# Half-tile staggered layer-norm pipeline, w1 in quarters, and segment sums taken from transposed pairs on VectorE

## The chip, the cores and the metric

The kernel runs on one core of one Trainium2 chip. The metric is the device time of one execution in microseconds (us), the median over several runs; smaller is better.

A core has five engines that work side by side, each in the order of its own instruction list: PE (TensorE, matrix products; its weight loads are shown apart as PEld), DVE (VectorE), ACT (ScalarE), POOL (GpSimd) and SP (SyncE, which here issues transfers). Transfers run on 16 DMA engines. Products are written to PSUM, a small memory that DVE and ACT read; everything else works in SBUF. An engine waits for another by a semaphore, and what stands behind a waiting instruction on the same engine waits as well.

## What is computed

The reference takes x (2048 tokens by 1024, bf16), normalises each token to xn, and adds two branches to x:

```python
xn = _layernorm(x)
return x + _A_ref(xn, A_mem0, A_Wq, A_Wk, A_Wv, A_Wo, A_seg_len) + _B_ref(xn, B_w1, B_w2, B_w3, B_w4)
```

Branch B is a mixer: h = gelu(layernorm(xn) @ w1); four groups of channels of h are shifted by one or two tokens and multiplied by w2; x1 = xn + that; then x1 + gelu(layernorm(x1) @ w3) @ w4, with 3584 inner channels.

Branch A is attention with 32 heads of 128 over segments of 32 tokens. Each segment is processed together with 8 memory rows, which are the output of the attention for the memory rows of the segment before it. So branch A is a recurrence over 64 segments. The kernel breaks it: it guesses the memory rows (attention is so flat here that a row's output is close to the mean of the values, which needs only the sum of xn over each segment, times Wv and Wo), runs all segments in parallel with the guess, and checks at the end that the guess agrees with the result within a tolerance. Otherwise a slow serial version runs.

## The kernel before

The order of the work on PE, SP and POOL is that of the program text all through; in the first two stages that of DVE and ACT is too. The line numbers here and in the profile are those of the kernel before. The stages, with the time at which PE does them in the profiled execution:

- **Stage 1, h = gelu(layernorm(xn) @ w1), 10.3 to 75.8 us.** The 2048 tokens are 16 tiles `n` of 128. SP loads x tiles (`load_x`, L226; a ring of 7) and w1 in two halves of 1 MB (L231) in the order x0, x1, half, x2, half, x3 to x6, then w2 (L236). For each tile, `norm_stats` computes mean and variance on DVE (two `bn_stats`, L249 and L252, `bn_aggr`, L253, and two small operations, L254 and L255), and POOL raises to the power of -1/2 (L256). `norm2` (L264) makes the doubly normalised tile on DVE for the first `NPE` = 8 tiles; these are transposed on PE (`transposes`, L283, four products with an identity per half tile) and copied from PSUM by ACT (L287) or, for the second half of tile 0, by DVE (L285). For tiles 8 to 15 ACT does `norm2` (L266) and SP transposes by DMA (L267). `norm1` (L273) makes xn, which POOL writes to a scratch tensor in DRAM (`xn_scratch`, L274). `seg_sums` (L292) then multiplies xn by a 128x4 matrix of ones to sum the segments of 32 tokens, eight products per tile on PE and a copy on ACT (L293). `stage1` (L300) makes for each of 8 output blocks `co` a sum of 8 products, and ACT applies gelu (L302); `between` hangs transposes, `prep` (norm2, statistics, norm1) and segment sums behind blocks `co`. It takes tile 0 alone, tile 1 alone, and then seven pairs. 13 products with a tile of zeros (L317) run ahead of all this.
- **Stage 2, the shifted product with w2 and the next layer norm, 75.9 to 131.1 us** (L387; DMA transposes at L400).
- **Stage 3, the two products with w3 and w4, 131.1 to 543 us.** Four blocks `tb` of 512 tokens: 28 blocks of channels against w3 (L523), then for each of 4 token tiles 56 products against w4 (L548) and an addition of R1 (L549), a tile that SP loads (`load_r1`, L514, L515) and to which POOL first adds x (L544). At its beginning SP issues m0 (the 8 memory rows, L412), the last four pieces of w3 (L205), w4 in seven pieces of 1 MB (L416), and the first R1. PE makes the guess of the memory rows in between: `mem_start` (L425, after block 20 of the first w3 pass) puts m0 in place and adds its rows' sum to that of segment 0; `unit_vb` (L440) multiplies 71 columns (8 copies for the first memory rows, 63 further segments) by Wv, `unit_g` (L454) by Wo, 256 products each.
- **Values for branch A (L579), 543 to 764 us, and attention, 764 us to the end**: projections (L652), scores (L667), outputs (L691), and the output projection `Out.piece` (L710), 32 products of 512 columns for each chunk, an addition on DVE (L716) and a store (L717). Eight chunks are left for the end; the last two are stored from SP.

Of the kernel before, what the change touches and what calls it, by code (L numbers as in the profile page):

```python
# [77 lines left out]
def kernel(  # L78
# [47 lines left out]
    segsum_np = np.zeros((P, 4), np.float32)  # L126
    for t in range(P):
        segsum_np[t, t // SEG] = 1.0
    segsum = const_tile("c_segsum", segsum_np)
# [54 lines left out]
    with tc.manual_schedule(engines={mybir.EngineType.PE, mybir.EngineType.SP, mybir.EngineType.Pool}), ExitStack() as actx:  # L184
# [6 lines left out]
        with ExitStack() as bctx:  # L191
            w3ctx = bctx.enter_context(ExitStack())
            xctx = bctx.enter_context(ExitStack())
            xsum = xctx.enter_context(tc.tile_pool(name="xs", bufs=1)).tile([P, KT, NSEG], BF16)
# [12 lines left out]
            with ExitStack() as hctx:  # L207
# [7 lines left out]
                with ExitStack() as p0:  # L215
# [13 lines left out]
                    load_x(1)  # L229
                    for c in range(2):  # L230
                        nc.sync.dma_start(w1_sb[:, :, c * 512:(c + 1) * 512], w1_v[:, :, c * 512:(c + 1) * 512])  # L231
                        load_x(c + 2)
                    for n in range(4, 7):
                        load_x(n)
# [54 lines left out]
                    def seg_sums(n, xn):  # L289
                        ps = psum0.tile([P, KT, 4], F32, tag="xs")  # L290
                        for k in range(KT):
                            nc.tensor.matmul(ps[:, k, :], xn[:, k * P:(k + 1) * P], segsum[:], start=True, stop=True)  # L292
                        nc.scalar.copy(xsum[:, :, 4 * n:4 * n + 4], ps[:])  # L293

                    def stage1(n0, nt, xn2T, between):
                        w = nt * P
                        for co in range(KT):
                            ps = psum.tile([P, 512], F32, tag="mm", bufs=4)
                            for k in range(KT):
                                nc.tensor.matmul(ps[:, :w].rearrange("p (n t) -> p n t", t=P), w1_sb[:, k, co * P:(co + 1) * P],  # L300
                                                 xn2T[:, :nt, k, :], start=(k == 0), stop=(k == KT - 1))
# [14 lines left out]
                    for i in range(13):  # L316
                        nc.tensor.matmul(ps[:], wz[:, :P], wz[:], start=(i == 0), stop=(i == 12))  # L317
                    norm_stats(0)
                    norm_stats(1, 0)
                    t0 = xn2T_tile()  # L320
                    xn2 = norm2(0, t0, 0)
                    transposes(xn2, t0, 0, 0)
                    transposes(xn2, t0, 0, 1, on_dve=True)
# [3 lines left out]
                    t1 = xn2T_tile()  # L327
                    xn2 = norm2(1, t1, 0)
                    norm_stats(2)

                    def first(xn2=xn2, t1=t1):
                        transposes(xn2, t1, 0, 0)
                        transposes(xn2, t1, 0, 1)
                    xns = {}

                    def sums_of(n):
                        if n in xns:
                            seg_sums(n, xns.pop(n))

                    stage1(0, 1, t0, {3: [first], 4: [lambda: norm_stats(3)]})  # L340
                    groups = [(1, 1)] + [(n, 2) for n in range(2, NT, 2)]
                    tiles2 = {1: t1}
                    xn2s = {}

                    def prep(n):
                        xn2s[n] = norm2(n, tiles2[n - n % 2], n % 2)
                        norm_stats(n + 2)
                        done = range(n - 2, n - 1) if n < NPE else range(NPE - 2, n + 1) if n == NPE else range(n, n + 1)
                        for m in done:
                            xns[m] = norm1(m)  # L350

                    def tr(n, half):
                        transposes(xn2s[n], tiles2[n - n % 2], n % 2, half)


                    for gi, (n0, nt) in enumerate(groups):
                        between = {c: [] for c in range(KT)}
                        if gi + 1 < len(groups) and groups[gi + 1][0] < NPE:
                            m0 = groups[gi + 1][0]
                            tiles2[m0] = xn2T_tile()  # L360
                            prep(m0)
                            between[1] += [lambda m0=m0: tr(m0, 0), lambda m0=m0: prep(m0 + 1)]
                            between[2] += [lambda m0=m0: tr(m0, 1)]
                            between[5] += [lambda m0=m0: tr(m0 + 1, 0)]
                            between[6] += [lambda m0=m0: tr(m0 + 1, 1)]
                        if gi + 2 < len(groups) and groups[gi + 2][0] >= NPE:
                            m0 = groups[gi + 2][0]
                            tiles2[m0] = xn2T_tile()
                            between[2] += [lambda m0=m0: prep(m0)]
                            between[5] += [lambda m0=m0: prep(m0 + 1)]  # L370
                        between[3] += [lambda n0=n0: sums_of(n0 - 1)]
                        between[4] += [lambda n0=n0: sums_of(n0 - 2)]
                        stage1(n0, nt, tiles2[n0], between)
# [443 lines left out]
        for o in rest[-2:]:  # L817
            o.last = True
# [178 lines left out]
```

## Time and profile before

| | us |
|---|---|
| median of 8 runs | 1530.63 |
| lowest, highest | 1529.32, 1531.52 |
| the profiled execution, its own time | 1529.74 |
| its span, first to last instruction | 1527.8 |
| PE busy (share of the span) | 1513.7 (99%) |
| DVE, ACT, POOL busy | 529.8, 506.6, 178.5 |
| mean granted TensorE clock | 0.998 of full |

The span is what the trace covers; 1.9 us of the execution's own time lie around it. Since PE is nearly always busy, the sums of the whole run say little: one has to look at the places where PE is idle, where its clock is down, and at what PE does that could be left out. A line of the timeline has start, duration, engine, line, operation, output <- inputs, and at its end, in square brackets, how long the engine had been idle and what ended that. Several instructions of one kind are merged (x8). The ends of products are modelled, so merged products can look some tenths of a us longer than their stream; the distance from one start to the next is the safer number. The chain of waits has start, duration, what. "SPq" is SP's issuing of transfers; the transfer itself comes later.

### The profile page before, as it was taken

How to read it: one execution, taken by the hardware profiler on the slowest of the kernel's cores; microseconds unless marked ns; L12 is line 12 of the kernel's file. 1: busy time of each engine (PE TensorE's matmuls, PEld its weight loads, DVE VectorE, ACT ScalarE, POOL GpSimd, SP SyncE). 2: the span in 40 equal slices, each digit the busy share in tenths (PEclk: the TensorE clock that was granted, in tenths of full speed). 3: DMA queues.
4: the chain of work that ended last, by engine and by line, in shares of the span. 5: the costliest groups of instructions: out<-in, count | busy, mean ns of one | idle time of the engine just before them, and what ended most of it. 6: DMA issues, size and time to landing. Idle time of an engine off the chain costs nothing.

```text
span 1527.8 us, 24314 instructions
## 1 busy us (share of the span) xinstructions
PE 1513.7 (99%) x9810; PEld 811.0 (53%) x9883; DVE 529.8 (35%) x1131; ACT 506.6 (33%) x1155; POOL 178.5 (12%) x248
## 2 busy tenths in 40 slices
PE   8999999999999999999999999999999999999998
PEld 7844444444444444444466645654665555445554
DVE  7284010000210122211146624650664266426641
ACT  5633202103012011111156614650663266326620
POOL 5232020221211222100000010001000100010001
PEclk9999999999999999999999999999999999999999
DMA  7779543452352877632499947992997398728711
GB/s 247 190 213 310 214 150 126 134 185 96 110 177 83 209 260 252 225 128 78 129 240 249 235 133 183 236 235 80 235 242 189 106 232 218 183 80 202 177 46 51
DMA packets 287373, 270.03 MB, mean 177 GB/s; under 512 B 136875, under 2 KB 255040, under 8 KB 287000
## 3 DMA queue, kind: packets, MB, share of 16 engines
q1 hardware_dynamic: 265208, 185.79, 47.1%
q0 software_dynamic: 22048, 82.63, 15.5%
q8 instruction: 80, 1.31, 0.4%
q14 instruction: 37, 0.30, 0.1%
HBM read 190.98 MB, written 46.19 MB: 155 GB/s over the span
## 4 chain that ended last, share of the span: by engine, by line
PE 98%; DMA 1%; DVE 0%; issue 0%; ACT 0%; SPq 0%
PE ps L652 30%; PE ps L579 14%; PE pso L710 14%; PE ps L523 13%; PE ps L548 13%; PE ps L387 4%; PE ps L300 3%; PE psS L667 2%; PE psO L691 2%; DMA xt<-in_A_x_dram 1%; PE ps L474 1%; PE ps L837 1%; PE gps L454 1%; PE ps L440 1%; PE ps L292 0%
## 5 line engine op out<-in xcount | busy, mean ns | idle before, releaser
L652 PE MATMUL ps<-hTb,wt 128*128 128x396 bf16 (+3 forms) x2560 | 509.5, 343 | 0.0
L652 PEld LDWEIGHTS <-wt 128*128 128x128 bf16 x2560 | 234.2, 98 | 166.1
L710 PE MATMUL pso<-wo_sb,oX 128*128 128x512 bf16 x1001 | 223.4, 379 | 1.3 <-issue 0.2
L579 PE MATMUL ps<-wt,xT 128*128 128x512 bf16 x1004 | 220.1, 379 | 1.1
L523 PE MATMUL ps<-xn3T,w_sb 128*128 128x512 bf16 x896 | 195.7, 379 | 0.0
L548 PE MATMUL ps<-w_sb,h3T 128*128 128x512 bf16 x872 | 194.3, 379 | 1.2
L579 PEld LDWEIGHTS <-xT 128*128 128x128 bf16 x1024 | 100.2, 98 | 120.8
L524 ACT ACTIVATE h3T<-ps 128x512 bf16<-128x512 f32 x112 | 66.8, 597 | 292.1 <-PE ps L523 291.2
L710 PEld LDWEIGHTS <-oX 128*128 128x128 bf16 x1024 | 98.8, 98 | 115.3
L658 ACT CAST KT<-ps 128x396 bf16<-128x396 f32 (+3 forms) x160 | 82.3, 514 | 223.7 <-PE ps L652 222.4
L548 PEld LDWEIGHTS <-h3T 128*128 128x128 bf16 x896 | 86.8, 98 | 102.8
L523 PEld LDWEIGHTS <-w_sb 128*128 128x128 bf16 x896 | 86.8, 98 | 102.7
L673 DVE TENSOR_REDUCE sums<-sm 99x4 f32<-99x396 f32 (+2 forms) x176 | 97.6, 555 | 113.5 <-ACT sm L671 113.5
L669 DVE TENSOR_TENSOR sm<-psS,c_mask_reg_sb 99x396 f32<-99x396 f32 x160 | 91.2, 570 | 90.0 <-PE psS L667 89.5
L671 ACT ACTIVATE sm<-sm 99x396 f32<-99x396 f32 (+2 forms) x176 | 92.8, 527 | 71.5 <-DVE sm L669 70.6
L581 ACT CAST Vs<-ps 128x512 bf16<-128x512 f32 x64 | 37.4, 587 | 233.2 <-PE ps L579 169.1
L660 ACT ACTIVATE QT<-ps 128x396 bf16<-128x396 f32 (+3 forms) x160 | 84.2, 526 | 74.1 <-PE ps L652 54.2
L585 DVE CAST Vs<-ps 128x512 bf16<-128x512 f32 x64 | 44.3, 692 | 170.0 <-PE ps L579 157.1
L549 DVE TENSOR_TENSOR R<-ps,R 128x512 f32<-128x512 f32 x32 | 22.1, 691 | 231.6 <-PE ps L548 220.7
L679 DVE TENSOR_TENSOR Pn<-sm,rs 99x396 bf16<-99x396 f32 (+2 forms) x176 | 98.9, 562 | 6.3 <-DVE rs L675 0.5
L692 ACT CAST oX<-psO 128x384 bf16<-128x384 f32 (+1 forms) x176 | 82.4, 468 | 8.3 <-PE psO L691 7.8
L717 POOL DMA_DIRECT2D out_dram<-ot x30 | 16.3, 545 | 583.4 <-DVE ot L716 577.5
(118 smaller groups left out, 980.1 us busy)
## 6 DMA issues: line engine op xcount, KB each, us to landing
wt<-in_A_Wk_dram SPq DMA_DIRECT2D x78, 512.0 KB
wt<-in_A_Wq_dram SPq DMA_DIRECT2D x76, 512.0 KB
wt<-in_A_Wv_dram POOLq DMA_DIRECT2D x24, 1024.0 KB, 6.7
V_scratch<-Vs SPq DMA_DIRECT2D x32, 512.0 KB
V<-V_scratch SPq DMA_DIRECT2D x32, 384.0 KB
w_sb<-in_B_w_dram SPq DMA_DIRECT2D x9, 1024.0 KB
R_scratch<-x POOLq DMA_DIRECT2D x16, 512.0 KB, 3.8
R<-R_scratch SPq DMA_DIRECT2D x16, 512.0 KB
```

The lines of the kernel that those rows point to most:

```text
L523: nc.tensor.matmul(ps[:].rearrange("p (n t) -> p n t", t=P), w3_sb[:, k, f * P:(f + 1) * P], xn3T[tb][:, :, k, :], start=(k == 0), stop=(k ...
L548: nc.tensor.matmul(ps[:], h3T[:, f, j * P:(j + 1) * P], w4_sb[:, f, ch * 512:(ch + 1) * 512], start=(f == 0), stop=(f == FT - 1))
L579: nc.tensor.matmul(ps[:], xT[:, m4 * 4 + j, k, :], wv[:, k, :], start=(k == 0), stop=(k == KT - 1))
L652: nc.tensor.matmul(ps[:, :nb] if flat else ps[:, :nb].rearrange("p (t c) -> p t c", t=nt), w[:, k, hh * P:(hh + 1) * P], B["rhs"](k), star ...
L658: nc.scalar.copy(o, i)
L660: nc.scalar.mul(o, i, scale)
L669: nc.vector.tensor_tensor(sm[:T, :, :T], S3, t["mask"][:].unsqueeze(1).to_broadcast((T, 4, T)), op=ALU.add)
L671: nc.scalar.activation(e[:T, :, :T], sm[:T, :, :T], ACTF.Exp, scale=LN2)
L673: nc.vector.tensor_reduce(ss, e[:T, :, :T], axis=AX.X, op=ALU.add)
L679: nc.vector.tensor_tensor(Pn[:T, :, :T], e[:T, :, :T], rs[:T, :].unsqueeze(2).to_broadcast((T, 4, T)), op=ALU.mult)
L692: nc.scalar.copy(oX[:, hs_, at:at + nt], O3[:, :, 0:nt])
L710: nc.tensor.matmul(self.ps[:], self.oX[:, h, self.gl * P:(self.gl + 1) * P], wo_sb[:, h, self.cc], start=(h == 0), stop=(h == H - 1))
```

## The change

1. **Order of the first eight tiles.** Statistics are split by half tile: the first `bn_stats` of tile n+1 now stands ahead of `norm2` of tile n on DVE, the rest behind it. Tiles 0 to 3 go through `stage1` one by one (before: 0 and 1), and pairs begin with tile 4. `norm1` of tile n-2 follows the statistics of n+1, for all tiles.
2. **The loads.** w1 comes in four quarters of 256 columns, in the order x0, quarter, x1, quarter, x2, quarter, quarter, x3 to x6. 15 products with zeros run ahead, not 13.
3. **The segment sums** leave stage 1 with their matrix of ones and the buffer `xsum`. In stage 3, SP transposes xn back from the scratch tensor by DMA, two tiles at a time, behind the pieces of w4 from the second on, and DVE sums over 32 tokens. Two buffers of the ring `R1` hold the pairs. m0 is loaded behind the first R1, and `mem_start` runs after the first token tile's product with w4.
4. **The guess** has 64 columns, one per segment, and the first one is copied to 8 places at the end.
5. **The last chunk** of the output projection is two of 256 columns. The last three chunks are stored from SP.

The core of the diff:

```diff
                     load_x(0)
-                    load_x(1)
-                    for c in range(2):
-                        nc.sync.dma_start(w1_sb[:, :, c * 512:(c + 1) * 512], w1_v[:, :, c * 512:(c + 1) * 512])
-                        load_x(c + 2)
-                    for n in range(4, 7):
+                    for c in range(4):
+                        nc.sync.dma_start(w1_sb[:, :, c * 256:(c + 1) * 256], w1_v[:, :, c * 256:(c + 1) * 256])
+                        if c < 2:
+                            load_x(c + 1)
+                    for n in range(3, 7):
                         load_x(n)
...
-                    def seg_sums(n, xn):
-                        ps = psum0.tile([P, KT, 4], F32, tag="xs")
-                        for k in range(KT):
-                            nc.tensor.matmul(ps[:, k, :], xn[:, k * P:(k + 1) * P], segsum[:], start=True, stop=True)
-                        nc.scalar.copy(xsum[:, :, 4 * n:4 * n + 4], ps[:])
...
-                    for i in range(13):
-                        nc.tensor.matmul(ps[:], wz[:, :P], wz[:], start=(i == 0), stop=(i == 12))
+                    for i in range(15):
+                        nc.tensor.matmul(ps[:], wz[:, :P], wz[:], start=(i == 0), stop=(i == 14))
...
+                    def tr(n, half, on_dve=False):
+                        transposes(xn2s[n], tiles2[n - n % 2], n % 2, half, on_dve)
+
                     norm_stats(0)
+                    norm2_of(0)
                     norm_stats(1, 0)
...
+                    tr(0, 0)
+                    tr(0, 1, True)
                     norm_stats(1, 1)
...
+                    for n in range(1, NPE):
+                        norm_stats(n + 1, 0)
+                        norm2_of(n)
+                        norm_stats(n + 1, 1)
+                        if n > 1:
+                            norm1(n - 2)
+                        if n < 4:
+                            stage1(n - 1, 1, tiles2[(n - 1) // 2 * 2], {5: [lambda n=n: tr(n, 0)], 6: [lambda n=n: tr(n, 1)]}, (n - 1) % 2)
+                    stage1(3, 1, tiles2[2], {4: [lambda: tr(4, 0)], 5: [lambda: tr(4, 1)], 6: [lambda: tr(5, 0)], 7: [lambda: tr(5, 1)]}, 1)
...
+                    for n0 in range(4, NT, 2):
                         between = {c: [] for c in range(KT)}
...
+                        if n0 + 4 < NT:
+                            between[2] += [lambda n0=n0: prep(n0 + 4)]
+                            between[5] += [lambda n0=n0: prep(n0 + 5)]
+                        if n0 == 4:
+                            for c in range(4):
+                                between[1 + 2 * c // 2 + (c > 1)] += [lambda c=c: tr(6 + c // 2, c % 2)]
+                        stage1(n0, 2, tiles2[n0], between)
...
+                def seg_sums(n):
+
+                    xr = ring.tile([P, 2, KT, P], BF16, tag="R1", name=f"xp{n}")
+                    for j in range(2):
+                        nc.sync.dma_start_transpose(xr[:, j], xn_v[:, n + j, :])
...
+                        for j in range(2):
+                            nc.vector.tensor_reduce(xb[:, :, 4 * (n + j):4 * (n + j) + 4], xr[:, j].rearrange("p k (s t) -> p k s t", t=SEG), axis=AX.X, op=ALU.add)
+
+                for c in range(8):
+                    if c < 7:
+                        nc.sync.dma_start(w4_sb[:, 4 * c:4 * (c + 1), :], w4_v[:, 4 * c:4 * (c + 1), :])
+                    if c > 0:
+                        seg_sums(2 * c - 2)
+                seg_sums(NT - 2)
...
                 load_r1(0)
+                m0 = ring.tile([M, D], BF16, tag="nsq", bufs=1)
+                nc.sync.dma_start(m0[:], A_mem0[0])
...
-                        if tb == 0 and f == 20:
-                            mem_start()
...
                         elif n > 0:
                             spec_step(depth)
+                        else:
+                            mem_start()
...
+        o = outs.pop()
+        outs += [Out(o.oX, o.gi, o.gl, c0, 256) for c0 in (512, 768)]
         head, rest = outs[:4], outs[4:]
...
-        for o in rest[-2:]:
+        for o in rest[-3:]:
             o.last = True
```

The products of `unit_vb` and `unit_g` take 64 columns in place of 71, and the tile of the guess is filled by four copies in place of two.

## The prediction

> **What bounds the kernel now.** I read the page first, for the span and the engine that fills it.
>
> ```profile
> span 1527.8 us, 24314 instructions
> ...
> PE 1513.7 (99%) x9810; PEld 811.0 (53%) x9883; DVE 529.8 (35%) x1131; ACT 506.6 (33%) x1155; POOL 178.5 (12%) x248
> ```
>
> PE bounds it. A gain can only be PE work left out, or PE idle or at low clock at the start or the end; a loss is any new wait of PE. So next the timeline of the first 24 us.
>
> ```profile
> 1.27 5.72 PE L317 MATMUL warm<-wz 128*128 128x512 bf16 x13 [1.27 <-DVE wz L311]
> ...
> 10.32 3.37 PE L300 MATMUL ps<-xn2T,w_sb 128*128 128x128 bf16 x32 [2.58 <-DMA w_sb<-in_B_w_dram]
> ...
> 14.19 2.84 PE L300 MATMUL ps<-xn2T,w_sb 128*128 128x128 bf16 x48
> 14.35 0.69 DVE L249 BATCH_NORM_STATS2 st<-xt 128x6 f32<-128x512 bf16 x1 [1.35 <-DMA xt<-in_A_x_dram]
> ...
> 17.09 0.61 PE L300 MATMUL ps<-xn2T,w_sb 128*128 128x128 bf16 x8
> ...
> 17.54 0.39 PE L283 MATMUL ps<-c_ident_sb,xn 128*128 128x128 bf16 x4
> ...
> 19.15 0.35 PE L292 MATMUL ps<-c_segsum_sb,xnk 128*128 128x4 bf16 x8 [0.78 <-DVE xnk L273]
> ```
>
> PE waits for the first half of w1 until 10.32 and for norm1 of tile 0 at 19.15. x3, loaded right behind the second half, is used at 14.35, so w1 is complete about 13.7 (an x tile takes 0.67 by the completion events). Starts give the prices: 8 products of 128 columns 0.45 (17.09 to 17.54); four transposes 0.22. The stretches by us show the clock:
>
> ```profile
> 10.00:11.00 1.00, 0.68 (x9) 0.68 (x10) 0.43 (x1) 0.00 (x0) 0.63 (x3) 0.80 1.08 389
> 11.00:12.00 1.00, 1.00 (x13) 1.00 (x11) 1.00 (x3) 0.28 (x1) 0.00 (x0) 0.50 1.07 397
> ...
> 14.00:15.00 1.00, 1.00 (x21) 1.00 (x19) 0.65 (x2) 0.85 (x2) 0.00 (x0) 0.99 1.06 412
> ```
>
> The clock (third number from the end) falls to half after the idle stretch and is back at 14, so the first 32 products take twice their time. Then the chain of waits, for the work that may go:
>
> ```profile
> 72.60 0.18 PE ps L292 x8
> 72.78 2.64 PE ps L300 x24
> 75.42 0.38 PE ps L292 x16
> ...
> 203.99 1.04 PE ps L440 x32
> ```
>
> Segment sums cost 0.18 per tile, 32 products of 71 columns 1.04. Last, SP's issues where the new transfers go, and the end:
>
> ```profile
> 139.96 17.58 SPq L416 DMA_DIRECT2D w_sb<-in_B_w_dram  x7
> 157.58 2.58 SPq L514 DMA_DIRECT2D R<-R_scratch  x1
> ...
> 497.34 6.35 SPq L543 DMA_TRANSPOSE xT<-xn_scratch  x4
> ...
> 1522.66 0.69 DVE L716 TENSOR_TENSOR ot<-pso,Rt 128x512 bf16<-128x512 f32 x1 [6.22 <-PE pso L710]
> ```
>
> SP is held back at 2.5 us for each MB of w4: the transfers are full there.
>
> **Part 1: up to the end of tile 0.** Before, tile 0 with the transposes of tile 1 ends at 14.19 + 32 x 0.056 = 16.0. After it, blocks 6 and 7 need the last quarter of w1. Ahead of that stand the same bytes as now (x0, x1, x2, w1), so it lands no sooner than 13.7. Packets of 512 B aren't in the trace; 1024 B take 46 ns and 2048 B 84 ns, a line that gives 27 ns (an estimate). Per DMA engine w1 is then 256 x 27 = 6.9 us in place of 128 x 46 = 5.9: it is complete at 14.7. Half a transpose and two blocks follow: 14.7 + 0.2 + 0.9 = 15.8. Against that stands the DVE order: the copy of tile 0's second half (0.69) stands behind the first statistics of x1 (0.69), and x1 now lands behind a quarter, so the first full block starts about 10 as before. I take 16.3, 0.3 us **lost**. A start at the full clock is hidden by the wait for w1. Bounds: 15.0 (packets at 23 ns, half of 46) and 25.6 (the 210 packets per us that the first half moved between 4 and 7 us, for all 4096).
>
> One rule that speaks against quarters is in the Trainium skill, "DMA: Bandwidth & Descriptors", section Bandwidth: load at least 1 MiB at once; its section on the anatomy of a DMA gives about 2.0 us fixed per transfer. Two more transfers would be 4 us by that (an estimate from the page), the sum +2.0. The trace has x tiles of 256 KB landing 0.67 apart, with no fixed cost between queued transfers, so I follow the trace.
>
> **Part 2: tile 1 to the end of stage 1.** Before: 75.88 - 16.0 = 59.9, of which products are 3.6 (a single) + 7 x 6.96 (pairs; 8 x 0.87) + 2.65 (twelve half transposes) + 2.9 (16 x 0.18, segment sums) = 57.9; 2.0 are gaps: 0.95 at 19.15, 0.2 at 38.77, the rest small. After: 3 x 3.6 + 6 x 6.96 + 2.65 = 55.2, plus 0.9 small gaps. New gaps come from ACT: transposes now stand behind blocks 5 and 6 of a single tile, and only 0.45 + 0.22 of PE work lies between the last and its use. On ACT two copies (starts 0.48 apart) and two gelus (0.2) have to pass: 0.2 late, three times; before tile 4, four copies and four gelus, 0.5; later 0.1. That is 1.2. DVE (2.8 per tile) stays ahead of PE (4.0). So 57.3, **2.6 saved**. Bounds: 1.0 (ACT gaps doubled, cover of the copies gone) to 3.8 (none).
>
> **Part 3: the guess.** 512 products at 64 columns: 128 columns take 56 ns, 71 take 32.5, so 0.41 per column and 2.9 ns each: **1.5 saved**. Four columns take 22 ns, so the weight path doesn't bind at 30. Bounds 0 and 1.9. Two more small copies on DVE stand in its idle time.
>
> **Part 4: the end.** The last addition shrinks from 0.69 to about 0.42 (284 columns take 0.45, L838); 64 products of 256 cost 0.06 more than 32 of 512. **0.2 saved**; bounds -0.5 and +0.1.
>
> **Part 5: pairs between the w4 pieces.** 16 transposes of 256 KB enter a full queue. The four from 497.34 land from 502.1 to 505.8, 1.2 apart: 2.4 per pair. The last w4 piece landed at 169.3; five pairs ahead of it make 181.3, and its first use is at 180.0 + 24 x 0.216 = 185.2: hidden, with 3.9 to spare. R1 comes some 23 us later; four PSUM buffers hide it until 204. What is not hidden is **m0**: it is issued behind eight pairs and R1, and PE stands at `mem_start` at 179.8 + 12.2 - 0.3 = 191.7 with everything queued behind it. From 180.1 POOL's 1 MB of Wv shares the engines (2.7, of which I charge 1.5): pair six lands at 181.3 + 2.4 + 1.5 = 185.2. The sums on DVE (1024 elements; 396 take 0.555, so 1.4) free its buffer at 186.6; only then SP issues pair eight, 3.2 (half of 6.35), and some 1.8 later it lands: 191.6. R1 and its x tile follow, 1.4 + 0.7: m0 at 193.7. PE waits **2.0**. Bounds: 0 (no sharing, sums at 1.1) and 7 (a pair at its issue price 3.2, 6 us over eight pairs, less what overlaps).
>
> The same page of the skill, section on latency and other measured facts, gives 261 GB/s for transposes. That would be 1.0 per tile (an estimate) and m0 in time: the sum would be -4.0. The trace's 1.2 decides.
>
> **Sum.** +0.3 - 2.6 - 1.5 - 0.2 + 2.0 = -2.0. The profiled execution's 1529.7 (span 1527.8, 1.9 around it) becomes 1527.7; it lies 0.9 below the median of the runs shown, so **1528.6** against 1530.6.
>
> **Rivals.**
> - *m0 is in time* (faster, 1526.6). For it: Wv may not slow the pairs, as SP's pace leaves holes in the queue late in the chain. Against: eight pairs are 19 us more in a full queue. Then -4.0. With the small gains of parts 1 and 2 at their good bounds, 1524. Chance 0.33.
> - *The pairs stop PE* (slower). If a transpose between copies costs its issue time, 1.6, not 1.2, a pair is 3.2: the last w4 piece lands at 185.3, and m0 near 200. PE waits 8 us at `mem_start`: -4.0 + 8 = +4, 1534.6. It decides from about 2.7 us per pair, where the gains are used up; at 3.1 it is slower by 3. For it: SP issues no faster than that. Against: the four after R1 landed 1.2 apart. Chance 0.12.
> - *Packets bind w1* (slower). If 512 B packets come at the early rate of 210 per us, a quarter lands as late as a half did, tile 0 ends at 25.6, and the sum is -2.0 + 9.3 = +7.3, 1537.9. The 340 per us seen after 9.5 speak against it. Chance 0.05.
> - *It doesn't start sooner.* The stagger and the quarters bring nothing at the start: that is in my forecast already.
>
> **How the numbers follow.** About 0.2% (3.1 us) is what a measurement of this kernel can tell from no change. The forecast, -2.0, has chance 0.50 and is within that. Faster by more, 0.33; slower by more, 0.17. The forecast's own range is 1527.5 to 1531.5. For 8 in 10 it reaches to the good case, 1525.5, and the first slow case, 1535.0; beyond lie the good bounds all together and the packets.
>
> **What would show it.** Right: products with w1 starting near 10, tile 0 done near 16, stage 2 starting near 73.6; 32 products of 64 columns in 0.95; a wait of PE for a DMA of m0 near 190, about 2 us. Wrong: stage 2 later than 75; PE waiting for w4; no wait at m0 (then faster); the last block of tile 0 later than 18; transposes in the queue farther apart than 1.4.

## The result, and the profile after

The changed kernel takes 1535.69 us (median of 14 runs), the kernel before beside it 1530.03: the ratio is 1.0044, with a 95% interval of 1.0034 to 1.0054. The change makes the kernel 5.7 us slower. The forecast was 1528.6, with a range up to 1535.0. The profiled execution of the changed kernel took 1534.64 us. Its page has the same picture as before, PE nearly always busy:

```profile
span 1532.8 us, 24293 instructions
...
PE 1511.3 (99%) x9781; PEld 809.4 (53%) x9853; DVE 548.1 (36%) x1148; ACT 506.7 (33%) x1147; POOL 179.0 (12%) x248
```

PE is busy 2.4 us less than before (1513.7) in a span that is 5.0 us longer. So PE now waits, and the waits of PE (in all, times, longest) say for what:

```profile
PE ps L410 <- DMA m<-in_A_mem_dram: 7.7, 1, 7.7
PE psO L675 <- DMA PT<-Pn: 2.1, 2, 1.1
PE ps L288 <- DMA w_sb<-in_B_w_dram: 1.4, 2, 1.0
...
PE ps L288 <- ACT xn2T L281: 0.8, 2, 0.5
```

The first line is `mem_start` waiting for m0. The second is attention waiting for transposed probabilities; the kernel before has no such wait. The timeline of PE at `mem_start`, and the stretches around it:

```profile
179.72 7.07 PE L531 MATMUL ps<-w_sb,h3T 128*128 128x512 bf16 x31
194.51 0.37 PE L410 MATMUL ps<-c_eye_sb,m 8*128 8x9 bf16 x8 [7.72 <-DMA m<-in_A_mem_dram]
194.81 14.81 PE L531 MATMUL ps<-w_sb,h3T 128*128 128x512 bf16 x55
209.46 1.10 PE L422 MATMUL ps<-xb,wt 128*128 128x64 bf16 x32
```

```profile
190.00:195.00 5.00, 0.49 (x9) 0.42 (x10) 2.35 (x2) 0.00 (x0) 0.00 (x0) 0.50 0.85 255
195.00:200.00 5.00, 5.00 (x13) 1.71 (x12) 1.52 (x4) 0.00 (x0) 2.78 (x3) 0.50 0.28 95
200.00:205.00 5.00, 5.00 (x25) 2.28 (x24) 0.69 (x1) 0.00 (x0) 2.07 (x1) 1.00 0.59 210
```

PE stops at 186.8 and goes on at 194.5. The clock (third number from the end) is then at half until 200: 13 products in the second stretch where the third has 25. The next 56 products take 14.7 us (194.88 to 209.62 in the chain of waits) instead of 12.2, so the wait costs 7.7 and another 2.5. The start of the program and the end of stage 1, in the same timeline:

```profile
1.26 5.46 PE L305 MATMUL warm<-wz 128*128 128x512 bf16 x15 [1.26 <-DVE wz L299]
...
8.10 2.06 PE L288 MATMUL ps<-xn2T,w_sb 128*128 128x128 bf16 x32 [0.45 <-ACT xn2T L281]
11.12 1.07 PE L288 MATMUL ps<-xn2T,w_sb 128*128 128x128 bf16 x16 [0.97 <-DMA w_sb<-in_B_w_dram]
...
12.87 0.62 PE L288 MATMUL ps<-xn2T,w_sb 128*128 128x128 bf16 x8 [0.46 <-DMA w_sb<-in_B_w_dram]
...
13.55 3.45 PE L288 MATMUL ps<-xn2T,w_sb 128*128 128x128 bf16 x56
```

The first full block starts at 8.10 and not at 10.32, it waits for ACT and not for w1, and its 32 products take 2.06 and not 3.37. The last quarter of w1 is there at 12.87; tile 0 ends at 13.55 + 0.45 = 14.0 (16.0 before), and stage 2 starts at 70.94 (75.88 before). The guess (chain of waits) and the end (timeline):

```profile
209.62 0.93 PE ps L422 x32
```

```profile
1525.56 0.42 DVE L700 TENSOR_TENSOR ot<-pso,Rt 128x256 bf16<-128x256 f32 x1 [2.80 <-PE pso L694]
1529.06 0.42 DVE L700 TENSOR_TENSOR ot<-pso,Rt 128x256 bf16<-128x256 f32 x1 [3.07 <-PE pso L694]
```

32 products take 0.93 instead of 1.04. From the last start of a projection to the end of the span it is 1532.8 - 1462.1 = 70.7 us, before 1527.8 - 1455.8 = 72.0.

So the difference of the two profiled executions can be put together, beside what the prediction had for each part:

| | forecast | measured |
|---|---|---|
| start of stage 2 | -2.3 | -4.9 |
| wait at `mem_start` | +2.0 | +7.7 |
| clock behind that wait | 0 | +2.5 |
| 64 columns in the guess (16 x 0.11) | -1.5 | -1.8 |
| projections: first to last start, 691.4 before, 693.8 after | 0 | +2.4 |
| the end | -0.2 | -1.3 |
| not assigned | | +0.4 |
| span | -2.0 | +5.0 |

### The profile page after: what moved, and what is told of

The parts are those of the page before. It is cut to its first block, busy times and chain, and to the rows that moved or that the text cites. A ratio compares the mean times of both kernels' runs of the same rounds, so it can differ in the third digit from the quotient of the medians.

```text
span 1532.8 us, 24293 instructions
## 1 busy us (share of the span) xinstructions
PE 1511.3 (99%) x9781; PEld 809.4 (53%) x9853; DVE 548.1 (36%) x1148; ACT 506.7 (33%) x1147; POOL 179.0 (12%) x248
## 4 chain that ended last, share of the span: by engine, by line
PE 92%; SPq 3%; DMA 2%; DVE 1%; issue 1%; ACT 0%; POOL 0%; POOLq 0%; DVEq 0%
PE ps L636 29%; PE pso L694 14%; PE ps L563 14%; PE ps L531 12%; PE ps L508 9%; PE ps L361 4%; SPq L395 2%; PE ps L288 2%; PE psS L651 2%; PE psO L675 2%; DMA PT<-Pn 1%; DMA xp<-xn_scratch 1%; PE ps L457 1%; PE ps L823 1%; PE gps L436 0%
## 5 line engine op out<-in xcount | busy, mean ns | idle before, releaser
L694 PE MATMUL pso<-wo_sb,oX 128*128 128x512 bf16 (+1 forms) x1034 | 223.6, 372 | 1.2 <-issue 0.2
L694 PEld LDWEIGHTS <-oX 128*128 128x128 bf16 x1056 | 101.9, 98 | 112.5
L655 ACT ACTIVATE sm<-sm 99x396 f32<-99x396 f32 (+2 forms) x176 | 92.7, 527 | 71.3 <-DVE sm L653 70.6
```

The source lines that it names most:

```text
L655: nc.scalar.activation(e[:T, :, :T], sm[:T, :, :T], ACTF.Exp, scale=LN2)
L694: nc.tensor.matmul(self.ps[:, :self.w], self.oX[:, h, self.gl * P:(self.gl + 1) * P], wo_sb[:, h, self.cc], start=(h == 0), stop=(h == H - 1))
```

## The experiments

The theory at this point: the change would have gained, and lost everything at `mem_start`, because m0 stands last in a queue that PE reaches before it is through. The rivals: the loss is in the transposes themselves wherever they stand, or in the sharing of the DMA engines with Wv, or in something of the new stage 1 or the layout. The table has all runs; "wait" is the longest wait of PE between 180 and 215, "proj" the time from the first to the last start of a projection, "V" the stage of values. `xb` is the tile of segment sums that `unit_vb` reads, R the tile in which POOL and DVE add up the result of branch B. Times in it come from one profile each, medians and ratios from the timed runs; each ratio is to runs of the kernel before on the same chip. The profiled executions of m0_first, m0_old_place and filled took 1531.44, 1529.89 and 1538.10, 3.3 to 3.9 above their medians, so their waits may be larger than is usual.

| run | median | ratio to before, 95% | stage 2 starts | wait | V starts | proj |
|---|---|---|---|---|---|---|
| before | 1530.03 | | 75.9 | none | 543.4 | 691.4 |
| the change | 1535.69 | 1.0034 to 1.0054 | 70.9 | 7.7 m0 | 547.3 | 693.8 |
| m0_first | 1528.11 | 0.9974 to 1.0011 | 71.2 | 3.6 xb | 542.6 | 695.3 |
| mem_later | 1531.94 | 1.0009 to 1.0031 | 71.6 | 4.7 xb | 544.3 | 693.9 |
| wv_later | 1532.12 | 1.0007 to 1.0035 | 70.6 | 5.1 m0 | 544.6 | 694.3 |
| three_bufs | 1536.81 | 1.0029 to 1.0060 | 72.3 | 9.8 m0 | 549.8 | 693.9 |
| m0_old_place | 1525.99 | 0.9962 to 0.9982 | 72.5 | 2.5 R | 541.2 | 695.1 |
| pe_sums | 1527.10 | 0.9967 to 0.9987 | 72.7 | none | 539.5 | 694.0 |
| stage1_alone | 1529.94 | 0.9988 to 1.0005 | 73.6 | none | 542.1 | 693.3 |
| tail_only | 1529.29 | 0.9984 to 1.0002 | 76.7 | none | 544.2 | 691.4 |
| before_shift | 1532.01 | 0.9999 to 1.0016 | 74.5 | none | 542.2 | 694.2 |
| pe_sums_shift | 1525.83 | 0.9957 to 0.9980 | 73.1 | none | 539.9 | 693.7 |
| halves (one run) | 1528.07 | | 72.9 | 0.8 w4 | 540.7 | 693.7 |
| pairs_late | 1543.82 | 1.0075 to 1.0111 | 72.2 | none | 538.2 | 692.6 |
| filled | 1534.49 | 1.0017 to 1.0054 | 72.5 | 4.0 m0 | 551.6 | 692.9 |
| pairs_late_steps | 1525.63 | 0.9955 to 0.9979 | 73.0 | none | 539.0 | 693.4 |

**m0_first: the load of m0 early, nothing else.**

```diff
                 w4_sb = big.tile([P, FT, D], BF16)
+                m0 = ring.tile([M, D], BF16, tag="m0", bufs=1)
+                nc.sync.dma_start(m0[:], A_mem0[0])
                 for _ in range(4):
                     load_w3()
...
                 load_r1(0)
-                m0 = ring.tile([M, D], BF16, tag="nsq", bufs=1)
-                nc.sync.dma_start(m0[:], A_mem0[0])
```

> Only the load of m0 is moved back to where it was, ahead of the last w3 pieces; everything else is the changed kernel. Theory (m0 stands behind the eight pairs and R1 in one queue, and PE waits for it at mem_start): the wait of 7.7 us goes, and with it the 2.5 us of half clock that follow it (13 us for the next products in place of 12.2 and more); the span falls from 1532.8 by some 10 to about 1522.6, below the kernel before by about 5. Rival (the crowded queue itself holds PE: without the wait for m0, the next thing late is R1 or the segment sums that unit_vb needs at 199): at most half of it comes back, the span stays at 1527 or more, and PE shows a wait between 187 and 212.

The wait at `mem_start` is gone, the median 7.6 us lower than that of the change, and no difference from the kernel before can be told. The theory's span of 1522.6 did not come (it is 1529.6); the rival's new wait did, one token tile further on. The chain of waits shows what it is made of:

```profile
193.90 5.45 DMA xr<-in_A_x_dram
...
199.56 2.13 POOL R L527
...
202.32 0.68 DVE R L532
203.00 0.13 DVE MZ L413
203.13 0.11 DVE xb L414
203.24 0.04 issue
203.29 1.86 PE ps L424 x32
```

The tile of x for the first addition of R lands behind the pairs; POOL adds it; DVE adds the products to R; and only behind those, in DVE's order, comes the small addition into xb for which PE waits with `vb`. The queue is late for R1 too, which m0 had hidden.

**mem_later: `mem_start` one token tile later, the transfers as in the change.**

```diff
-                        else:
-                            mem_start()
...
                         elif n > 0:
+                            if n == 1:
+                                mem_start()
                             spec_step(depth)
```

> m0 stays late in the queue; only mem_start stands one token tile later on PE, right ahead of the first unit_vb, at about 199. No transfer changes. Theory: m0 lands at 194.5 as before, PE doesn't wait, span as in the kernel with m0 loaded first, 1522 to 1524, clock full throughout. Rival (the loss is contention of the pairs with what PE reads, not the wait): no change from 1532.8.

m0 is in time, and the same addition into xb holds PE 4.7 us. Neither number came: the span is 1529.8. So the place of `mem_start` alone doesn't save the change.

**wv_later: the first tile of Wv behind `mem_start`, so that POOL's transfer doesn't meet the pairs.**

```diff
                     if tb == 0:
-                        spec_load()
...
                             mem_start()
+                            spec_load()
```

> m0 stays late; the first Wv tile (1 MB, issued by POOL) is loaded after mem_start and not at 175. Theory (that load takes the DMA engines packet for packet, 4096 B against 256 B, which is why pair six took 5.4 us from its first to its second half): pair six is 3.5 to 4 us faster, m0 lands near 191, PE's wait shrinks from 7.7 to about 4, span 1528 to 1529 if the clock still drops and 1526 if it doesn't. Rival (the pairs are limited by SP's issue and by the sums on DVE alone): wait unchanged within 1 us.

By the completion events (the trace's marks of a transfer having landed), the second half of pair six lands 2.4 us behind the first (180.05 to 182.49) and not 5.4 (180.0 to 185.4 in the change), and m0 at 191.5 instead of 194.5. Against the profile of the change the sharing is worth 3 us of the queue. 5.1 us of wait are left without it, where about 4 were expected.

**three_bufs: a third buffer in the ring of the pairs.**

```diff
-                    xr = ring.tile([P, 2, KT, P], BF16, tag="R1", name=f"xp{n}")
+                    xr = ring.tile([P, 2, KT, P], BF16, tag="R1", bufs=3, name=f"xp{n}")
```

> The ring R1 has three buffers in place of two, so SP waits for the sums of the pair before the last but one. Theory (the chain is bound by the transfers and the Wv load, the ring adds about 2 at its end): the eighth pair lands 1.5 to 3 us sooner, R1 and m0 as much, PE waits 5 to 6, span about 1530 to 1531. Rival (the ring of two is what paces the pairs): all pairs come sooner, m0 lands before 189 and the wait falls below 2.

Neither number came: the wait is 9.8 us and m0 lands at 198.0. By the completion events, what is late is pair six beside the Wv transfer: it ends 8.6 us behind the last w4 piece (181.0 to 189.6), where the change has 6.4 and wv_later 3.5. In m0_first, m0_old_place and filled it is 9.3 to 10.8. Behind pair six the third buffer does help: pair eight ends 4.8 us later, and 5.9 to 6.3 in the other runs with these pairs. So the ring of two costs some 1.1 to 1.5 us, and the meeting with Wv decides more; why it takes so unlike times is not shown.

**m0_old_place: m0 early and `mem_start` back behind block 20 of w3.**

```diff
+                        if tb == 0 and f == 20:
+                            mem_start()
                         if tb > 0 and f % 7 == 6:
...
-                        else:
-                            mem_start()
```

> The change, with the load of m0 queued ahead of the last w3 pieces and mem_start back in its old place after block 20 of w3, so that the addition into xb is behind the eight pairs' sums on DVE and ahead of the additions of R; the pairs stay where the change put them. Theory of the queue: what the change lost is the wait at mem_start, the clock that fell behind it and, once m0 is early, the wait for the addition into xb behind the additions of R; with all three gone nothing at mem_start or vb, at most 1 us at the third token tile of w4 for its buffer, the clock full from 185 to 210, V starting near 538 instead of 547.3, median near 1525.5 (1524 to 1527). Rival, the queue is late as a whole: the pairs still bring R_scratch's first tile in near 199 and PE waits 3 us or more for it, at one place or another, with the clock below 0.9: V near 541.5, median 1528 to 1529, as when only the load was early.

The addition into xb now runs between the sums, and `vb` doesn't wait. The waits of PE:

```profile
PE psO L675 <- DMA PT<-Pn: 3.2, 3, 1.3
PE ps L533 <- DVE R L534: 2.5, 1, 2.5
```

R is what is left of the late queue, 2.5 us. The median, 1525.99, lies where the theory of the queue put it; the forecast of 1 us at most for R was too low, and V, at 541.2, is nearer the rival's 541.5, in an execution that is 3.9 above the median. By the median this version beats both kernels. The clock stays full behind 2.5 us without work:

```profile
200.00:205.00 5.00, 2.45 (x40) 1.61 (x39) 1.29 (x2) 0.00 (x0) 2.12 (x1) 1.00 0.47 157
205.00:210.00 5.00, 4.95 (x24) 2.28 (x24) 1.62 (x3) 0.00 (x0) 3.60 (x3) 1.00 0.33 117
```

**pe_sums: the sums back on PE, without pairs.** `seg_sums` as in the kernel before; four tiles' sums stand in stage 2.

```diff
-                for c in range(8):
-                    if c < 7:
-                        nc.sync.dma_start(w4_sb[:, 4 * c:4 * (c + 1), :], w4_v[:, 4 * c:4 * (c + 1), :])
-                    if c > 0:
-                        seg_sums(2 * c - 2)
-                seg_sums(NT - 2)
+                for c in range(7):
+                    nc.sync.dma_start(w4_sb[:, 4 * c:4 * (c + 1), :], w4_v[:, 4 * c:4 * (c + 1), :])
```

> The change without its last part: the segment sums go back to 128 products on PE with xsum, four token tiles' sums of them in stage 2, no pairs on the queue, m0 early and mem_start in its old place; the new stage 1, the 64 columns and the divided last piece stay. Theory: the pairs are what lost; the sums on PE cost 2.7 us, stage 1, 64 columns and the end keep their gains, so V starts near 539.5 (543.4 less 4.8 and 1.75, plus 2.7), no wait at mem_start or vb. If the 2.4 us that the attention part lost (waits for PT) go with the layout that the removed constant and pool changed, proj takes 691.4 as before and the median is near 1524.5; if they go with anything else of the change, proj takes 693.8 and the median is near 1527.

V starts at 539.5, as forecast. Without the pairs the other parts of the change are a gain, 0.2% against the kernel before. The attention loses its 2.4 us here too, with the old constant and the old pool in place, so the removed objects aren't the reason.

**stage1_alone and tail_only: the kernel before with one part each.** The first has the loads, the 15 products and the order of stage 1; the second has

```diff
+        o = outs.pop()
+        outs += [Out(o.oX, o.gi, o.gl, c0, 256) for c0 in (512, 768)]
         head, rest = outs[:4], outs[4:]
...
-        for o in rest[-2:]:
+        for o in rest[-3:]:
```

> The kernel before with the new stage 1 alone (quarters of w1, 15 warm products, tile by tile for the first four tiles), the segment sums on PE, four tiles' sums of them in stage 2. Theory: the stage gives 4.8 less the 2.7 us of the sums, some 2.1 us, which stay to the end: V near 541.3, median near 1528 with proj at 691.4, or 1530 if the waits for PT come here too. Rival, the gain of stage 1 is given back at w4 because the load of w4 binds there: V near 543.4, median 1530.

> The kernel before with the last piece of the output in two of 256 columns, three stored from SP, nothing else. Theory: the end after PE's last product is shorter by 1.1 to 1.4 us, median near 1528.9 against 1530; by the recorded estimate 0.2, so 1529.8. If the waits for PT in the attention part come from the longer list of output pieces, they show here, 2 us or more, and the median is over 1530.5.

Stage 1 alone gives 2.3 us (75.9 to 73.6) with the segment sums still on PE, and 1.3 of it are left at V. At the end they are gone: the projections take 693.3 and PE waits 1.6 us for PT. So the attention's loss comes with the new stage 1 alone, where no transfer, buffer or constant of the attention differs. The end alone takes 70.8 us behind the last projection, 1.2 less than before, with proj at 691.4. The intervals of both medians hold 1, so these sizes rest on the profiles.

**before_shift and pe_sums_shift: only PE's count of instructions moved.** The trace of the change has transfers of 16384 B in the queue that carries instructions, one per 256 of PE's instructions and each taking 0.9 to 1.7 us in this part; two of them start at 806.6 and 821.5, and PE waits for PT until 810.8 and 824.4. In the kernel before, the first projection is PE's instruction 45 of a block of 256; in each run with a changed stage 1 up to here it was 177.

```diff
-                    for i in range(13):
-                        nc.tensor.matmul(ps[:], wz[:, :P], wz[:], start=(i == 0), stop=(i == 12))
+                    for i in range(79):
+                        nc.tensor.matmul(ps[:, :84], wz[:, :P], wz[:, :84], start=(i == 0), stop=(i == 78))
```

> The kernel before with its 13 warm products of 512 columns made 79 of 84 columns (same columns in sum, 132 more instructions on PE), nothing else. Theory of the phase: PE's instructions are fetched 256 at a time by a 16 KB transfer that takes 1.0 to 2.0 us on one of the DMA engines that also carry PT; where such a fetch falls decides the waits for PT, and 132 more instructions put the fetches where the changed kernels have them. So waits for PT of 1.5 to 3 us between 764 and 850, proj takes 693.3 to 694.5 instead of 691.4, median 1532.4. Rival, the waits come from something else that the change carries: none here, proj 691.4, median 1530.3.

> The kernel with the segment sums back on PE, its 15 warm products of 512 columns made 77 of 100 columns (20 columns more in sum, 124 more instructions on PE: the place within 256 that the kernel before has at the first product of the attention part). Theory of the phase: no waits for PT, proj 691.4 instead of 694.0, median 1524.7. Rival: waits as before the padding, 2.3 us, proj 694, median 1527.1.

The kernel before with 66 more small products at its start waits in the attention, 800 us later:

```profile
PE psO L691 <- DMA PT<-Pn: 2.5, 2, 2.0
```

Its projections take 694.2. So the wait comes without any of the change's work. That the count of instructions brings it rests on this one profile: V starts 1.2 us earlier here too, and the interval of the median holds 1. The way back holds only in part: with the old place within 256, pe_sums_shift waits 1.2 instead of 2.3 us for PT and 0.6 for weights, and proj is 693.7, hardly less. The phase of PE's fetches seems to matter; it isn't all, and what else does stays open.

**halves: m0_first with w1 in two halves again.**

```diff
-                    for c in range(4):
-                        nc.sync.dma_start(w1_sb[:, :, c * 256:(c + 1) * 256], w1_v[:, :, c * 256:(c + 1) * 256])
...
+                    load_x(1)
+                    for c in range(2):
+                        nc.sync.dma_start(w1_sb[:, :, c * 512:(c + 1) * 512], w1_v[:, :, c * 512:(c + 1) * 512])
+                        load_x(c + 2)
```

> The change with m0 early, w1 loaded in two halves in the order of the kernel before (x1 ahead of w1, x2 and x3 between and behind), everything else of the new stage 1 kept. Theory: what made stage 1 4.8 us shorter instead of the forecast 2.3 is the early first quarter: it lets full blocks start at 8.1, when PE has idled 2.6 us, and the clock stays at 1.00. With halves the first full block starts near 10.3, PE idles over 4 us, the clock is near 0.5 from 10.6 to 14, tile 0 is done near 16 and stage 2 starts near 73.3 (71.2 with quarters). Rival, the quarters with their shorter packets are no help: start and stage 2 as with quarters, 8.1 and 71.2.

Neither number came, the theory's less wrong than the rival's. The timeline:

```profile
9.02 1.96 PE L288 MATMUL ps<-xn2T,w_sb 128*128 128x128 bf16 x32 [1.11 <-DMA w_sb<-in_B_w_dram]
12.80 1.07 PE L288 MATMUL ps<-xn2T,w_sb 128*128 128x128 bf16 x16 [1.82 <-DMA w_sb<-in_B_w_dram]
...
14.60 3.45 PE L288 MATMUL ps<-xn2T,w_sb 128*128 128x128 bf16 x56
```

The first full block starts 0.9 later than in m0_first, and tile 0 ends at 14.60 + 0.45 = 15.05 instead of 14.3: in these profiles the quarters are worth 0.8 up to there. The rest of the later stage 2 can't be put down to the halves: a wait of 1.5 for a DMA transpose of xn2 stands in it, and runs with quarters have such waits too (1.0 in three_bufs, 1.3 in filled). The clock stays full with halves. The first half landed at 9.0 here and at 8.9 in before_shift, not at 10.3. But tail_only, whose start is that of the kernel before, has both the late half and the half clock:

```profile
9.82 3.27 PE L300 MATMUL ps<-xn2T,w_sb 128*128 128x128 bf16 x32 [2.45 <-DMA w_sb<-in_B_w_dram]
```

```profile
10.00:11.00 1.00, 1.00 (x12) 1.00 (x11) 0.81 (x2) 0.11 (x1) 0.26 (x3) 0.50 1.10 402
```

So they don't belong to halves as such, nor to one execution alone; what makes the half late is not shown.

**filled: products in the wait.** Their result isn't used.

```diff
                 def mem_start():
+                    junk = psum3.tile([P, 512], F32, tag="g", name="junk")
+                    for i in range(34):
+                        nc.tensor.matmul(junk[:], w3_sb[:, 0, :P], w3_sb[:, 0, :512], start=(i == 0), stop=(i == 33))
```

> The change with 34 products of 512 columns (0.22 us each, 7.4 us, their result is not used) on PE ahead of m0's products, in the place of the wait at mem_start; transfers unchanged. Theory of the clock: the wait costs itself (7.7 us) and, by the clock at 0.50 from 190 to 200, 2.5 us more; with PE kept busy the clock stays at 1.00, m0's products start at 194.5 as in the change, vb at 207.0 instead of 209.5, V near 544.8 instead of 547.3, median near 1533.2 instead of 1535.7. Rival, the clock falls for another reason (the load on the engines, the transposes): 0.5 at 190 to 200 with or without the products, V at 547 or later.

The queue ran 5 us later in this profile (m0 at 199.7), so the numbers for `vb` and V can't be used, and the median, 1534.49, can't be told from that of the change. The clock can be used:

```profile
190.00:195.00 5.00, 5.00 (x25) 2.25 (x23) 3.47 (x3) 0.00 (x0) 0.00 (x0) 1.00 0.69 146
195.00:200.00 5.00, 1.00 (x13) 0.42 (x11) 2.35 (x2) 0.00 (x0) 0.00 (x0) 1.00 0.85 226
200.00:205.00 5.00, 4.88 (x16) 1.92 (x17) 1.52 (x4) 0.00 (x0) 2.36 (x2) 0.66 0.37 143
```

It is full while PE works, with the same transfers under way, and it falls only behind the 4.0 us that are left of the wait. So in this profile PE's idleness takes the clock down, and the load on the DMA engines doesn't.

**pairs_late and pairs_late_steps: the transposes where nothing waits.** m0 early, w4 in one run, then R1 and the transposes, one token tile each through two small buffers:

```diff
                 load_r1(0)
+                for n in range(8):
+                    seg_sums(n)
...
                         load_r1(n + 1)
+                        if n < 2:
+                            for m in range(8 + 4 * n, 12 + 4 * n):
+                                seg_sums(m)
```

with `mem_start` behind the third token tile. Both runs also have the 77 warm products of pe_sums_shift, and so the old place within 256. The second run also has two more steps for the units of the guess:

```diff
-                        if tb > 0 and f % 7 == 6:
+                        if tb > 0 and f % 7 == 6 or tb == 3 and f in (3, 10):
```

> The change with m0 early, the w4 pieces in one run, R_scratch's and x's first tile next, and the 16 transposes behind them one token tile at a time through two small buffers: eight, four behind the second tile's loads, four behind the third's; mem_start after the third token tile, vb from the fourth; warm products as 77 of 100 columns. Theory of the queue: nothing waits at mem_start, vb or w4, so the new stage 1, the 64 columns and the removed sums keep all their gain: V near 537 (539.5 with the sums on PE, less 2.7), proj 691.4, median near 1522. Rival, the transposes hold back R's second or third tile or the units of the guess are late at the end of the last token tile: a wait of 2 us or more appears there, V 539.5 or later, median 1525 or more.

> The kernel with the transposes behind the w4 pieces, one token tile at a time, with two more steps for the units of the guess in the last w3 stage (after blocks 3 and 10). Theory of the queue: the 13.7 us ahead of V go, nothing else waits, V near 538, stage of V 221 us, proj 691.4 to 693.8, median 1522 to 1524.5, faster than both kernels. Rival, the extra steps wait for their weights (PE waits in the w3 stage, 2 us or more): V 540 or later, median 1525 or more.

In the first, no wait stands in w4, but the guess has two steps fewer and its last units come late: PE waits 13.7 us in the stage of V.

```profile
PE ps L561 <- ACT Vs L563: 13.7, 1, 13.7
```

With the two steps back that wait is gone and the kernel is at 1525.63, 0.2 to 0.45% faster than before. That is 1.1 above the upper end of what was expected: stage 2 starts at 73.0 in this profile, with a wait of 1.4 us for ACT behind the many small products, and the projections take 693.4. No wait of PE in this profile is put down to the transposes; what cost in the change was their place. m0_old_place, pe_sums_shift and pairs_late_steps can't be told from each other.

## Why the prediction was wrong

The step that failed is in part 5: "m0 at 193.7. PE waits **2.0**". The mechanism was right, the sizes weren't. Stage 1 gave PE and the queue 4.9 us, so each forecast time is moved by that; the measured ones are completion events of the trace:

| landing | forecast | moved by 4.9 | measured |
|---|---|---|---|
| last w4 piece | 181.3 | 176.4 | 179.0 |
| pair six | 185.2 | 180.3 | 185.4 |
| pair eight | 191.6 | 186.7 | 191.5 |
| m0 | 193.7 | 188.8 | 194.5 |
| PE at `mem_start` | 191.7 | 186.8 | 186.8 |

PE came exactly when it was forecast to, and m0 5.7 us late: 2.6 us up to the last w4 piece, 2.5 us at pair six, 0.6 behind it. SP's issues show the first term.

```profile
150.20 5.01 SPq L395 DMA_TRANSPOSE xp<-xn_scratch  x2
155.26 0.58 SPq L402 DMA_DIRECT2D w_sb<-in_B_w_dram  x1
156.00 5.06 SPq L395 DMA_TRANSPOSE xp<-xn_scratch  x2
161.11 0.58 SPq L402 DMA_DIRECT2D w_sb<-in_B_w_dram  x1
161.81 5.59 SPq L395 DMA_TRANSPOSE xp<-xn_scratch  x2
...
173.99 15.24 SPq L395 DMA_TRANSPOSE xp<-xn_scratch  x6
189.34 0.51 SPq L497 DMA_DIRECT2D R<-R_scratch  x1
...
190.37 0.37 SPq L502 DMA_DIRECT2D m<-in_A_mem_dram  x1
```

A pair and a piece are issued every 5.8 to 6.3 us; from the first of them to the last, by the landings, it is (179.0 - 149.7) / 5 = 5.9. The forecast had 2.4 + 2.7 = 5.1. The rival "The pairs stop PE" named this: at 3.2 per pair PE waits 8 us at `mem_start` and the kernel is at 1534.6. It had a chance of 0.12 and is what happened, in its place and nearly in its size (of the wait; the clock behind it was not in it); the price per pair that it needed is 5.9 - 2.7 = 3.2. What it had wrong is the reason. The two halves of a pair land 0.8 to 1.0 apart, less than my 1.2; the rate for transposes in the Trainium skill ("DMA: Bandwidth & Descriptors", section on latency and other measured facts), which I set aside in part 5, was nearer. It is the w4 piece behind each pair that took 3.6 to 4.5 us in four of five cases. My price was for a stream of transposes; the change alternates them with plain transfers. Why these come slower in the alternation is not shown.

The second term: while POOL's 1 MB of Wv is under way (179 to 182.5) SP's queue moves 84 packets of 256 B per us against 500 to 1000 when it has the engines to itself, and Wv moves 84 of 4 KB. I charged 1.5 us for it; wv_later shows 3.0, and in three_bufs, m0_first, m0_old_place and filled pair six takes another 2.3 to 4.4. The Trainium skill says in "DMA: Bandwidth & Descriptors", section on queues, rings and completion order, that an engine takes turns between queues packet by packet. The count of one to one agrees in the change, and against 4 KB packets the queue with 256 B packets loses. (The page's packet holds several descriptors; whether it is the trace's packet is not shown.) In filled Wv's queue moves only 9 to 43 packets per us as well, from 181 to 191, and one to one doesn't explain that.

The third thing was not in the prediction: **the clock**. The start of the program had shown that it falls behind an idle stretch, and I did not carry that over to the wait I forecast. It cost 2.5 us more.

The other steps:

- *Part 1* (0.3 lost) was wrong in sign: tile 0 ends at 14.0, 2.0 earlier. I let the first full block start "about 10 as before". The first quarter lands early enough for 8.10, and w1 is complete by 12.87, where I had 14.7. The price of a packet was right (27 ns in the median); what failed is the 13.7 to which I added 1.0. That was itself late: in two halves, w1 is complete by 12.8 in the run `halves` and by 12.5 in before_shift. "A start at the full clock is hidden by the wait for w1" failed with it. Some of the 2.0 belongs to the late landing of the first half in the profile of before (10.3, and 9.8 in tail_only, against 8.9 in before_shift, whose stage 2 starts 1.4 earlier), so how much part 1 is worth in the median stays open. The fixed 2.0 us per transfer that the prediction set aside stands in the Trainium skill, "DMA: Bandwidth & Descriptors", section on the anatomy of one DMA, for transfers that GpSimd issues; SP issues those of w1.
- *Part 2* (2.6 saved) held: from 14.0 to 70.94 it is 56.9, where 57.3 was forecast (3.0 saved).
- *Part 3* (1.5 saved) held: 0.93 per 32 products for a forecast of 0.95.
- *Part 4* (0.2 saved) was too small. The forecast addition of 0.42 came, but I counted the addition alone: from its end to the end of the span it is now 3.3 us instead of 4.5, behind a store of half the size. In all 1.2 to 1.3 us.
- *The attention* was costed at nothing, and lost 2.4. This wasn't foreseen at all. before_shift loses as much with none of the change's work in it; but pe_sums_shift, pairs_late and pairs_late_steps, with the old place within 256, still lose 1.2 to 2.3, so the cause stays open.
- *The range* ended at 1535.0. It took in the rival's 1534.6 without the clock or the attention behind it.

## What to carry to other kernels

Put a small load that an in-order engine will wait for ahead of a long row of transfers, and look for who else stands at the end of that row: here R1 behind m0. When a forecast holds a wait of PE of some 2.5 us or more, allow for the clock: here a wait of that length once left it full and twice halved it. And before believing a change of 2 us in one stage, move the program by a few instructions and see whether a stage that wasn't touched moves as much.

## What the runs showed of the hardware that was not expected

- **Idle time and the clock.** Behind a PE wait of 2.5 us the clock stayed at 1.00 (m0_old_place). With a wait of 3.6 us it was 0.81 and 0.85 in the stretch of 5 us in which the wait ended and the next (m0_first), with 4.7 us 0.69 and 0.63 (mem_later), with 7.7 us 0.50 in both (the change), and behind 4.0 us 0.66 in one (filled). The Trainium skill, "TensorE: Matmul & The Clock Gate", section on what is actually happening, names an idle window of about 3.4 us and two states only. These rows lie on both sides of it; the values between are means of a stretch. The start of the program doesn't fit: behind waits of 2.58 us (the kernel before) and 2.45 us (tail_only) the clock fell to 0.50, with only eight small products between the warm-up and the wait.
- **Fetches of instructions ride on the same DMA engines.** The profile lists their queue among those of the 16 engines, and the trace has a 16384 B transfer for each 256 instructions of PE, as the Trainium skill says of the blocks in "Runtime: NRT & Kernel Launch", section on instruction fetch mechanics. The page calls crossing a block mostly hidden. Here such a fetch takes up to 2.6 us (filled), and transfers near one are late: pair six ends at 185.4 in the change with a fetch at 183.3 to 184.3, and PT comes late in the attention. That the fetch delays them is argued from its place in the trace; before_shift shows only that the wait for PT comes without the change's work.
- **A ring of two buffers cost less than the transfer beside it.** With a third, pair eight ended 4.8 us behind pair six and not 5.9 to 6.3 (three_bufs). But pair six ended 6.2 to 10.8 us behind the last w4 piece with the Wv transfer beside it and 3.5 without (wv_later).
